# One scalar folded into the operations of a bias network, early loads moved, and the last sums cut in halves

## The chip, the cores and the metric

The kernel runs on one core of a Trainium2 chip. The metric is the device time of one execution in microseconds (us), as the median of several runs; less is better. The engines are TensorE (PE in the rows; its weight loads PEld), VectorE (DVE), ScalarE (ACT), GpSimd (POOL) and SyncE (SP), which issues nearly all transfers here.

## The reference

Attention with 4 batches, 8 heads, 576 positions and a head width of 64, in float32, with a learned bias on the scores; its output goes through two feed-forward layers. Cut to what matters here:

```python
scores = q @ k.T / sqrt(64)
x = log1p(abs(i - j)) / log1p(max(i, 1))           # per pair of positions
h = maximum(x[..., None] * w1 + b1, 0)             # 32 hidden units
scores += (h @ w2).transpose(2, 0, 1)              # one bias per head
attn = softmax(scores) @ v                         # then (2304, 512) tokens
x1 = hardswish(attn @ moe_w_in) @ moe_w_out        # 512 -> 2048 -> 512
out = sigmoid(x1 @ w_gate) * (x1 @ w_val) @ w_out  # 512 -> 1536 -> 512
```

## The kernel before

The bias stage comes first. The hidden layer is worked out on 128 partitions, 32 hidden units for each of four neighbouring rows i. `tbl` holds log1p of the distance; it is loaded in two pieces, the far one (columns `NEAR` on, 640 columns, needed first) and the near one (511 columns). `mlpc` holds w1, b1 and w2, `rows` the values of log1p(i) (`psi`) and 8 over it. L445 multiplies the two pieces of the table by w1 in place. L446 and L447 make `bpsi`, b1 times psi, with both signs. Dividing x by psi is put off: max(w1 * table + b1 * psi, 0) is the hidden value times psi. There are 36 groups `G` of 16 rows, each with four operations over 576 columns, one for each `ct`. In five of six groups the first of the four is done by ScalarE (L482, Relu with a bias per partition); the others are done by VectorE (L484, the maximum of the table and minus b1 * psi, with a correction `corr`, L459, added later). The results go round a ring of 12 buffers (`hids`), so that an operation of group G waits for the matmuls of group G - 3. TensorE multiplies by w2 (L489) into one of four PSUM tiles. `bias_out` then scales by 8 / psi and adds `corr` on ScalarE (L467) into one of three `p` buffers, and after every second group SP writes the pair to DRAM (`nbias`, L470). When all rows of a block of 128 are written, SP loads that block for the first pair of heads (`load_bias`, L219; the fifth, short block in two pieces, `bias_m`, L221 and L222). Three warm-up matmuls (L438) read a zeroed piece of the first ring buffer.

The attention has 16 units (pair of heads and batch), each with 9 steps; two steps make a slot (`slot_of_two`). A step forms scores on TensorE (L262), adds the bias on VectorE (L266), takes exp on ScalarE (L282, into the same three `p` buffers), and turns the result on TensorE (L320); later slots multiply by v (`av`, L352) and scale. The operands of the scores are split in a high and a low part by `prep`: for unit 0 it is ScalarE (casts, L230) and VectorE (L238), called within the bias stage behind groups 4 and 12; for the others ScalarE casts q (L230), and GpSimd rounds k (L234) and forms both low parts (L238). q and k of a unit are loaded by `load_qk` (L209 and, for the two halves of k, L211) into one buffer, so a load waits until `prep` has read the unit before. For unit 1 it is called behind the last group, after the last `nbias` write; for unit n + 1 later, a step after the second half of `prep` for unit n.

The feed-forward layers follow, with TensorE as the busy engine; the weights stream in behind it. At the very end three blocks of 128 rows are summed with the other half of the layer (L664, 512 columns) and written (L665), each as soon as its matmuls are through.

The planner of the framework chooses the order of the instructions of each engine within what they need of each other; `issue_after` is the one means by which the program fixes an order on a queue.

Of the kernel before, what the change touches and what calls it, by code (L numbers as in the profile page):

```python
# [13 lines left out]
AF = mybir.ActivationFunctionType  # L14
ALU = mybir.AluOpType
# [3 lines left out]
P = 128  # L19
# [7 lines left out]
TW = 384  # L27
# [6 lines left out]
ND, NPSI = 2 * S - 1, S // 4 + S // 16  # L34
NEAR = S - 65
# [60 lines left out]
def block_kernel(ctx: ExitStack, tc: tile.TileContext, q, k, v, mlp, w_in, w_out, w_gate, w_val, w_out2, dist_d,  # L96
                 rows_d, out):
    nc = tc.nc
# [9 lines left out]
    nbias = [dram.tile([min(P, S - P * c), H, S], F32, name=f"nbias{c}") for c in range(5)]  # L108
# [83 lines left out]
    q_in, k_in, bpsi, mlpc, rows = [early[:, i:j] for i, j in zip(cut, cut[1:])]  # L192
    k_in, bpsi = [a.rearrange("p (h s) -> p h s", h=2) for a in (k_in, bpsi)]
    bias_t = [apool.tile([P, 2, S], F32, name=f"bias{c}") for c in range(4)]
    bias_m = apool.tile([P, S], F32, name="bias_m")
# [8 lines left out]
    w1c, b1c, w2bd = mlpc[:, 0:1], mlpc[:, 1:3], mlpc[:, 3:35]  # L204
    corr = apool.tile([P, 2], F32, name="corr")

    def load_qk(n):
        qn[n], kn[n] = q_in[0:D], k_in
        nc.sync.dma_start(qn[n], q[n])  # L209
        for r in range(2):  # L210
            nc.sync.dma_start(kn[n][D * r : D * r + D], k[n])  # L211

    def load_v(n):
        vn[n] = a2.tile([P, 10, D], F32, name="vn")
        return nc.sync.dma_start(vn[n], v[n])

    def load_bias(p, c):
        if c < 4:
            nc.sync.dma_start(bias_t[c], nbias[c][:, 2 * p : 2 * p + 2, :])  # L219
        else:  # L220
            nc.sync.dma_start(bias_m[0:64], nbias[4][:, 2 * p, :])  # L221
            nc.sync.dma_start(bias_m[64:P], nbias[4][:, 2 * p + 1, :])  # L222

    def prep(n, h, on=PREP_ON):

        Q, K, qt, kt = Qs[n % 2][:, QH[h]], Ks[n % 2][:, :, h], qn[n][:, QH[h]], kn[n][:, h]

        def high(eng, out, x):
            if eng == "A":
                nc.scalar.copy(out, x)  # L230
            elif eng == "V":
                nc.vector.tensor_copy(out, x)
            else:
                nc.gpsimd.tensor_tensor(out=out, in0=x, in1=one[0 : x.shape[0]].to_broadcast(x.shape), op=ALU.mult)  # L234

        def low(eng, out, x, hi):
            eng = nc.vector if eng == "V" else nc.gpsimd
            eng.tensor_tensor(out=out, in0=x, in1=hi.bitcast(F32), op=ALU.subtract)  # L238

        high(on[0], Q[0:D], qt)  # L240
        high(on[1], K[:, 0], kt)
        low(on[2], Q[D:P], qt, Q[0:D])
        low(on[3], K[:, 1], kt, K[:, 0])
# [123 lines left out]
    for n in range(NU):  # L367
        i = (NSTEP * n + 5) // 2 + 2
        j = max(i + 2, (NSTEP * n + 8) // 2 + 2)
# [7 lines left out]
    def slot_of_two(i):  # L377

        for t in steps(i):
            scores(t)  # L380
            n, s = seq[t]
            p, b = divmod(n, B)
            if s == 0:
                last_v[0] = load_v(n)
            if b == B - 1 and p + 1 < NPAIR and (s % 2 == 1 or s == 8):
                load_bias(p + 1, s // 2)
        for n, a, g in AV.get(i, ()):
            av(n, a, g)
            if g == 4:
                av_out(n, a)  # L390
        for t in steps(i):
            expo(t)
        for t in steps(i - 1):
            n, s = seq[t]
            if s in (5, 8):
                invert(n, s // 6 * 3, s // 6 * 2 + 3)
        for t in steps(i - 2):
            n, s = seq[t]
            if s in (5, 8):
                turn_inv(n, s // 6 * 3, s // 6 * 2 + 3)  # L400
        for t in steps(i - 1):
            trans(t)
            n, s = seq[t]
            if s in REM:
                trans_rem(n, REM[s])
        for t in steps(i):
            if t in PREP:
                n, h = PREP[t]
                prep(n, h)
            for k, (n, h) in PREP.items():  # L410
                if h == 1 and n + 1 < NU and t == k + 3:
                    load_qk(n + 1)

    PREP = {}
    for n in range(1, NU):
# [3 lines left out]
    with ExitStack():  # L419

        tbl = x1[3][:, 0:ND]
        hids = [x1[i][:, S * j : S * j + S] for i in range(3) for j in range(4)]
        psi, rpsi8 = rows[:, 0 : S // 4], rows[:, S // 4 : NPSI]
        nc.sync.dma_start(mlpc, mlp)
        nc.sync.dma_start(rows, rows_d)
        nc.sync.dma_start(tbl[:, NEAR:ND], dist_d[:, NEAR:ND])
        nc.sync.dma_start(tbl[:, 0:NEAR], dist_d[:, 0:NEAR])

        warm = x1[0][:, 0:512]
# [11 lines left out]
        for i in range(2):  # L441
            nc.gpsimd.memset(Pm[i][:, 0:64], 0.0)

        for r in (slice(NEAR, ND), slice(0, NEAR)):
            nc.vector.tensor_scalar(out=tbl[:, r], in0=tbl[:, r], scalar1=w1c, scalar2=None, op0=ALU.mult)  # L445
        nc.vector.tensor_scalar(out=bpsi[:, 0], in0=psi, scalar1=b1c[:, 0:1], scalar2=None, op0=ALU.mult)  # L446
        nc.vector.tensor_scalar(out=bpsi[:, 1], in0=psi, scalar1=b1c[:, 0:1], scalar2=-1.0, op0=ALU.mult,  # L447
                                op1=ALU.mult)
# [7 lines left out]
        for ct in range(4):  # L456
            r = slice(32 * ct, 32 * ct + 32)
# [4 lines left out]
        def bias_out(G, ps):  # L462
            if G % 2 == 0:
                evs[0] = a2.tile([P, 2, S], F32, name="p", bufs=3)
            ev = evs[0]
            b = corr[:, 1:2] if G % ACT_SKIP == ACT_SKIP - 1 else corr[:, 0:1]
            nc.scalar.activation(halves(ev[:, G % 2]), ps[:, :, 0:HS], AF.Identity, bias=b, scale=rpsi8[:, G : G + 1])  # L467
            if G % 2 == 1:
                c, r = divmod(16 * (G - 1), P)
                last_b[0] = nc.sync.dma_start(nbias[c][r : r + 32].rearrange("(g i) h j -> (i h) g j", g=2), ev)  # L470
                if r == P - 32 or G == S // 16 - 1:
                    load_bias(0, c)
# [3 lines left out]
        for G in range(S // 16):  # L476
            hid = [hids[(4 * G + ct) % 12] for ct in range(4)]
            for ct in range(4):
                qd = 4 * G + ct
                src = tbl[:, S - 1 - 4 * qd : 2 * S - 1 - 4 * qd]  # L480
                if ct == 0 and G % ACT_SKIP != ACT_SKIP - 1:
                    nc.scalar.activation(hid[ct], src, AF.Relu, bias=bpsi[:, 0, qd : qd + 1], scale=1.0)  # L482
                else:
                    nc.vector.tensor_scalar(out=hid[ct], in0=src, scalar1=bpsi[:, 1, qd : qd + 1], scalar2=None,  # L484
                                            op0=ALU.max)
            ps = bp.tile([P, 2, 512], F32, name="s")
            for a in range(2):
                for ct in range(4):
                    nc.tensor.matmul(ps[32 * ct : 32 * ct + 32, a, 0:HS], w2bd, hid[ct][:, HS * a : HS * a + HS],  # L489
                                     start=True, stop=True)  # L490
            if pend is not None:
                bias_out(*pend)
            pend = (G, ps)
            if G in (4, 12):
                prep(0, G // 12, "AAVV")
        bias_out(*pend)
        with tc.issue_after(last_b[0].ins):
            load_qk(1)

        def split_x(x):  # L500
            for c in range(4):
# [133 lines left out]
        for j, (part2, t) in enumerate(todo):  # L635
            os = [mp.tile([P, 512], F32, name=f"o{c}") for c in range(NB)]
            prev = None
            for e in range(NH * part2, NH * part2 + NH):
                while load.done < 2 * NF + 3 * e + 3:
                    load.tick()  # L640
                s0 = 2 * NF + 3 * e
                pg = project(slots[s0 % NALL])
                pv = project(slots[(s0 + 1) % NALL])
                g = moe.tile([P, TW], F32, name="g", bufs=2)
                nc.scalar.activation(g, pg, AF.Sigmoid)  # L645
                nc.vector.tensor_tensor(out=g, in0=g, in1=pv, op=ALU.mult)  # L646
                gg = split_g(g)
                if prev is not None:
                    out2(e - 1, prev, os, e - 1 == NH * part2, False, False)
                prev = gg  # L650
                freed = 2 * NF + 3 * NH * part2
                if t == NTILE - 1:
                    freed += 3 * (e - NH * part2)
                if e % NH < NH - 2:
                    go_on(freed, 68)
            if j + 1 < len(todo):
                split_x([X2[:, c] for c in range(4)])
                if j + 2 < len(todo):
                    X2 = take(x2[todo[j + 2][1]])
            out2(NH * part2 + NH - 1, prev, os, False, True, j == len(todo) - 1)  # L660
            for i in range(NB):
                o = acc[NB * t + i]
                if part2:
                    nc.vector.tensor_tensor(out=o, in0=o, in1=os[i], op=ALU.add)  # L664
                    nc.sync.dma_start(out[TW * t + P * i : TW * t + P * i + P, :], o)  # L665
                else:
                    evac("AV"[i % 2], o, os[i])

# [26 lines left out]
```

## Time and profile before

| | |
|---|---|
| median of 3 runs | 1209.4 us (1208.53 to 1209.43) |
| profiled execution | 1207.13 us |
| its span | 1205.4 us |
| TensorE busy | 1187.5 us, 99% of the span |
| VectorE / ScalarE / GpSimd busy | 57% / 48% / 11% |
| granted TensorE clock | full in all 40 slices of the span |
| bias stage, first to last L484 | 5.59 to 59.43 us |
| last sum begins / span ends | 1201.65 / 1205.4 us |

Busy shares are averages over stages with different limits, and a busy TensorE is not one at its peak, since its matmuls overlap. So the stages are read one by one: in each, the engine whose rows follow each other with no idle time sets the length, and the others have room. A row of the timeline has start and duration, and several like instructions in a row are drawn together, with their count; the bracket behind it gives idle time of the engine before it and what ended it.

### The profile page before, as it was taken

What the parts mean: (1) busy time and instruction counts of PE and PEld (TensorE: products, weight loads), DVE (VectorE), ACT (ScalarE), POOL (GpSimd) and SP (SyncE); (2) the same over time, 40 slices, a digit from 0 to 9 for tenths busy, and PEclk for the clock granted to TensorE, in tenths of its full rate; (3) what the DMA queues carried; (4) which work ended last, traced back from release to release, by engine and by line L of the source; (5) the groups of instructions that cost most, each with busy time, mean ns of one, the idle gap of its engine ahead of it and who ended that gap; (6) DMA issues with size and microseconds to landing.
All of it is one profiled execution on the core that took longest, in us unless ns stands there. A gap on an engine that the chain in (4) does not pass through costs nothing.

```text
span 1205.4 us, 18764 instructions
## 1 busy us (share of the span) xinstructions
PE 1187.5 (99%) x7302; PEld 1057.4 (88%) x7302; DVE 682.1 (57%) x1464; ACT 574.2 (48%) x1224; POOL 133.2 (11%) x108
## 2 busy tenths in 40 slices
PE   8989999999999999999999999999999999999998
PEld 3467777777789999999999999999999999999998
DVE  8967887778876555645565545564431544222332
ACT  7978877877854444434344434333321332221221
POOL 0055545544200000000000000000000000000000
PEclk9999999999999999999999999999999999999999
DMA  6643635353211232212222223322210121101000
GB/s 210 244 141 105 186 100 178 110 164 108 76 53 67 92 105 80 79 62 80 74 69 82 92 88 114 122 80 79 64 58 1 62 79 53 53 1 53 27 27 27
DMA packets 36152, 106.76 MB, mean 89 GB/s; under 512 B 3936, under 2 KB 10336, under 8 KB 36064
## 3 DMA queue, kind: packets, MB, share of 16 engines
q1 hardware_dynamic: 36064, 105.57, 26.9%
q8 instruction: 57, 0.93, 0.3%
q14 instruction: 31, 0.25, 0.1%
HBM read 80.78 MB, written 24.77 MB: 88 GB/s over the span
## 4 chain that ended last, share of the span: by engine, by line
PE 87%; DVE 6%; ACT 3%; DMA 2%; issue 1%; POOL 0%; SPq 0%; DVEq 0%; ACTq 0%
PE o L574 16%; PE h L512 13%; PE h L510 13%; PE h L511 13%; PE o L631 12%; PE s L262 6%; PE av L352 5%; PE tr L320 4%; PE s L489 1%; PE av L355 1%; DVE u L266 1%; DVE x L484 1%; DVE z L143 1%; ACT p L282 1%; PE tr L299 1%
## 5 line engine op out<-in xcount | busy, mean ns | idle before, releaser
L510 PE MATMUL h<-early,slot 128*128 128x384 f32 x952 | 318.9, 335 | 0.0
L512 PE MATMUL h<-early,slot 128*128 128x384 f32 x952 | 318.8, 335 | 0.0
L511 PE MATMUL h<-early,slot 128*128 128x384 f32 x952 | 318.5, 335 | 0.0
L510 PEld LDWEIGHTS h<-early,slot 128*128 128x128 f32 x952 | 178.8, 188 | 2.6
L511 PEld LDWEIGHTS h<-early,slot 128*128 128x128 f32 x952 | 178.7, 188 | 2.5
L512 PEld LDWEIGHTS h<-early,slot 128*128 128x128 f32 x952 | 178.7, 188 | 0.1
L551 ACT CAST gh<-g 128x384 fp32r<-128x384 f32 x166 | 85.0, 512 | 162.4 <-DVE g L646 119.8
L574 PE MATMUL o<-gh,slot 128*128 128x384 f32 x768 | 156.9, 336 | 3.0 <-ACT raw L310 1.8
L646 DVE TENSOR_TENSOR g<-g,h 128x384 f32<-128x384 f32 x72 | 39.8, 553 | 183.1 <-PE h L512 183.1
L574 PEld LDWEIGHTS o<-gh,slot 128*128 128x128 f32 x768 | 134.2, 188 | 6.9 <-ACT raw L310 4.4
L552 DVE TENSOR_TENSOR gl<-g,gh 128x384 fp32r<-128x384 f32 x166 | 92.2, 558 | 79.1 <-ACT gh L551 77.0
L516 ACT ACTIVATE g<-h,half 128x384 f32<-128x384 f32 x94 | 54.5, 580 | 131.1 <-PE h L512 127.5
L262 PE MATMUL s<-k,q 128*128 128x288 f32 x640 | 112.2, 310 | 2.5 <-POOL k L234 1.2
L645 ACT ACTIVATE g<-h 128x384 f32<-128x384 f32 x72 | 35.4, 492 | 165.0 <-PE h L512 165.0
L282 ACT ACTIVATE p<-u,stat 128x576 f32<-128x576 f32 x128 | 98.7, 773 | 28.9 <-DVE stat L266 28.5
L631 PE MATMUL o<-slot,gh 128*128 128x512 f32 x432 | 111.9, 393 | 0.0
L266 DVE CUSTOM_DVE_ANT_0 u<-s,bias 128x576 f32<-128x576 f32 x128 | 93.5, 753 | 24.9 <-PE s L262 24.3
L517 DVE SCALAR_TENSOR_TENSOR g<-g,h 128x384 f32<-128x384 f32 x94 | 51.8, 552 | 95.2 <-ACT g L516 95.1
L262 PEld LDWEIGHTS s<-k,q 128*128 128x128 f32 x640 | 89.0, 189 | 5.9 <-POOL k L234 1.7
L631 PEld LDWEIGHTS o<-slot,gh 128*128 128x128 f32 x432 | 80.1, 188 | 13.6 <-issue 0.2
L574 PE MATMUL o<-gl,slot 128*128 128x384 f32 x384 | 88.5, 334 | 0.0
L352 PE MATMUL av<-ptm,vn 128*64 128x288 f32 x512 | 78.9, 419 | 1.2 <-DVE x L359 0.7
(99 smaller groups left out, 1494.0 us busy)
## 6 DMA issues: line engine op xcount, KB each, us to landing
raw<-in_part_dram SPq DMA_DIRECT2D x68, 512.0 KB, 3.5
nbias<-p SPq DMA_DIRECT2D x18, 576.0 KB, 3.2
early<-in_part_dram SPq DMA_DIRECT2D x32, 288.0 KB, 4.3
bias<-nbias SPq DMA_DIRECT2D x16, 576.0 KB, 6.0
take<-x SPq DMA_DIRECT2D x12, 768.0 KB, 4.1
vn<-in_part_dram SPq DMA_DIRECT2D x16, 320.0 KB, 3.1
early<-in_part_dram SPq DMA_DIRECT2D x16, 304.0 KB, 3.8
part<-raw SPq DMA_DIRECT2D x12, 384.0 KB, 2.6
```

What stands on the lines that cost most here:

```text
L262: nc.tensor.matmul(ps[:, a, 0:HS], Q[:, q0 : q0 + P], K[:, r, h, HS * a : HS * a + HS], start=(i == 0), stop=(i == len(mm) - 1))
L266: last_u[0] = nc.vector.tensor_tensor_reduce(out=halves(u), in0=ps[:, :, 0:HS], in1=halves(bt), op0=ALU.add, op1=ALU.min, scale=-0.125, sc ...
L282: nc.scalar.activation(probs(t), us.pop(t), AF.Exp, bias=low[n % 2][:, s : s + 1], scale=-1.0, accum_out=sums[n % 3][:, s : s + 1])
L352: nc.tensor.matmul(ps[64 * h : 64 * h + 64, 0:HS], vt[:, 4 * h + g], ptm[:, h, g, cols], start=(g == 0), stop=False)
L510: nc.tensor.matmul(ps[:, 0:TW], wh, XH[:, c], start=(c == 0), stop=False)
L511: nc.tensor.matmul(ps[:, 0:TW], wl, XH[:, c], start=False, stop=False)
L512: nc.tensor.matmul(ps[:, 0:TW], wh, XL[:, c], start=False, stop=(c == 3))
L516: nc.scalar.activation(g, ph, AF.Relu, bias=half, scale=1.0 / 6.0)
L551: nc.scalar.copy(gh, g)
L552: last_g[0] = nc.vector.tensor_tensor(out=gl, in0=g, in1=gh.bitcast(F32), op=ALU.subtract)
L574: nc.tensor.matmul(os[c][:, 0:TW], sl[:, r, P * c : P * c + P], x, start=(first and r == 0 and x is gh), stop=(last and x is gl))
L631: nc.tensor.matmul(os[i], x[:, P * i : P * i + P], sl[:, r], start=(first and x is gh and r == 0), stop=(end and x is gl))
```

## The change

The two multiplications L445 are taken out. w1 becomes the scale of ScalarE's Relu (L482) and the first of two operations in VectorE's L484: multiply by w1, then take the maximum; both read w1 as a scalar per partition, beside the one that they read already. `mlpc` and `rows` are loaded from ScalarE's queue, and the far piece of the table is the first load on SP. q and k of unit 1 are loaded at group 31, behind the latest `nbias` write issued by then (that of groups 28 and 29). The later calls of `load_qk` are held behind the second half of the latest load of `bias_m`. In the last tile each sum and its write are made in two halves of 256 columns.

```diff
+    last_m = [None]
     def load_bias(p, c):
...
-            nc.sync.dma_start(bias_m[64:P], nbias[4][:, 2 * p + 1, :])
+            last_m[0] = nc.sync.dma_start(bias_m[64:P], nbias[4][:, 2 * p + 1, :])
...
                 if h == 1 and n + 1 < NU and t == k + 3:
-                    load_qk(n + 1)
+                    with tc.issue_after(last_m[0].ins):
+                        load_qk(n + 1)
...
-        nc.sync.dma_start(mlpc, mlp)
-        nc.sync.dma_start(rows, rows_d)
         nc.sync.dma_start(tbl[:, NEAR:ND], dist_d[:, NEAR:ND])
+        nc.scalar.dma_start(mlpc, mlp)
+        nc.scalar.dma_start(rows, rows_d)
         nc.sync.dma_start(tbl[:, 0:NEAR], dist_d[:, 0:NEAR])
...
-        for r in (slice(NEAR, ND), slice(0, NEAR)):
-            nc.vector.tensor_scalar(out=tbl[:, r], in0=tbl[:, r], scalar1=w1c, scalar2=None, op0=ALU.mult)
...
-                    nc.scalar.activation(hid[ct], src, AF.Relu, bias=bpsi[:, 0, qd : qd + 1], scale=1.0)
+                    nc.scalar.activation(hid[ct], src, AF.Relu, bias=bpsi[:, 0, qd : qd + 1], scale=w1c)
                 else:
-                    nc.vector.tensor_scalar(out=hid[ct], in0=src, scalar1=bpsi[:, 1, qd : qd + 1], scalar2=None,
-                                            op0=ALU.max)
+                    nc.vector.tensor_scalar(out=hid[ct], in0=src, scalar1=w1c, scalar2=bpsi[:, 1, qd : qd + 1],
+                                            op0=ALU.mult, op1=ALU.max)
...
+            if G == 31:
+                with tc.issue_after(last_b[0].ins):
+                    load_qk(1)
         bias_out(*pend)
-        with tc.issue_after(last_b[0].ins):
-            load_qk(1)
...
                 if part2:
-                    nc.vector.tensor_tensor(out=o, in0=o, in1=os[i], op=ALU.add)
-                    nc.sync.dma_start(out[TW * t + P * i : TW * t + P * i + P, :], o)
+                    for c in (slice(0, 256), slice(256, 512)) if j == len(todo) - 1 else (slice(0, 512),):
+                        nc.vector.tensor_tensor(out=o[:, c], in0=o[:, c], in1=os[i][:, c], op=ALU.add)
+                        nc.sync.dma_start(out[TW * t + P * i : TW * t + P * i + P, c], o[:, c])
```

## Rows read from the trace of the kernel before

**Rows 1.** The page, busy time of TensorE (us, share of the span, instructions).

```profile
PE 1187.5 (99%) x7302; PEld 1057.4 (88%) x7302; DVE 682.1 (57%) x1464; ACT 574.2 (48%) x1224; POOL 133.2 (11%) x108
```

**Rows 2.** Stretches: length, busy (instructions) per engine, clock, DMA share, GB/s.

```profile
70.90:84.00 13.10, 10.83 (x64) 6.63 (x64) 5.34 (x15) 7.91 (x21) 9.27 (x8) 1.00 0.45 113
110.60:118.40 7.80, 7.80 (x63) 5.69 (x64) 6.07 (x16) 6.11 (x17) 7.15 (x6) 1.00 0.08 12
```

**Rows 3.** Timeline of VectorE, 2 to 60 us: start, duration, engine, line, operation, count.

```profile
5.00 0.55 DVE L445 TENSOR_SCALAR x<-x,early 128x640 f32<-128x640 f32 x1 [1.08 <-DMA x<-in_part_dram]
...
6.03 0.49 DVE L445 TENSOR_SCALAR x<-x,early 128x511 f32<-128x511 f32 x1
...
7.21 0.66 DVE L459 TENSOR_SCALAR corr<-s 32x1 f32<-32x1 f32 x4 [0.26 <-PE s L454]
7.90 5.68 DVE L484 TENSOR_SCALAR x<-x,early 128x576 f32<-128x576 f32 x13
...
27.96 31.47 DVE L484 TENSOR_SCALAR x<-x,early 128x576 f32<-128x576 f32 x73
```

**Rows 4.** Timeline of VectorE, from 352 us: two operations with immediates alone.

```profile
352.34 0.75 DVE L141 TENSOR_SCALAR z<-z 128x512 int32<-128x512 int32 x2
353.01 1.29 DVE L143 SCALAR_TENSOR_TENSOR z<-raw,z 128x512 int32<-128x512 int32 x2
```

**Rows 5.** Timeline of ScalarE, 14 to 20 and 68 to 70 us.

```profile
15.56 1.43 ACT L482 ACTIVATE x<-x,early 128x576 f32<-128x576 f32 x2
...
18.93 1.54 ACT L467 ACTIVATE p<-s,corr,early 128x576 f32<-128x576 f32 x2
...
68.42 0.58 ACT L310 COPY ptm<-tr 128x512 f32<-128x512 f32 x1
68.90 0.26 ACT L310 COPY ptr<-tr 128x128 f32<-128x128 f32 x1
69.05 0.67 ACT L230 CAST q<-early 64x576 fp32r<-64x576 f32 x1
69.63 0.78 ACT L282 ACTIVATE p<-u,stat 128x576 f32<-128x576 f32 x1
```

**Rows 6.** Groups by line and form: busy us, mean ns, idle before.

```profile
L664 DVE TENSOR_TENSOR x<-x,o 128x512 f32<-128x512 f32 x16 | 10.1, 683 | 9.3 <-PE o L631 9.3
```

**Rows 7.** Timeline of SP, 0 to 110 us: issues of transfers.

```profile
0.74 0.38 SPq L424 DMA_DIRECT2D early<-in_part_dram  x1
...
1.64 0.42 SPq L426 DMA_DIRECT2D x<-in_part_dram  x1
...
51.79 7.64 SPq L470 DMA_DIRECT2D nbias<-p  x4
...
67.16 0.46 SPq L221 DMA_DIRECT2D bias_m<-nbias  x1
...
68.30 1.24 SPq L211 DMA_DIRECT2D early<-in_part_dram  x2
```

**Rows 8.** Timeline of GpSimd, 60 to 90 us.

```profile
73.35 2.25 POOL L234 TENSOR_TENSOR k<-early,one 128x576 fp32r<-128x576 f32 x2 [1.76 <-DVE stat L288]
75.56 2.77 POOL L238 TENSOR_TENSOR k<-early,k 128x576 fp32r<-128x576 f32 x2
```

**Rows 9.** Timeline of TensorE, 68 to 120 us: matmuls with v.

```profile
70.89 0.70 PE L352 MATMUL av<-ptm,vn 128*64 128x288 f32 x2 [0.53 <-DVE ptm L312]
...
84.04 1.68 PE L352 MATMUL av<-ptm,vn 128*64 128x288 f32 x12
...
110.55 1.68 PE L352 MATMUL av<-ptm,vn 128*64 128x288 f32 x12
...
118.32 1.68 PE L352 MATMUL av<-ptm,vn 128*64 128x288 f32 x12
```

**Rows 10.** One line of the kernel, L288: duration in ns, least, median and most.

```profile
L288 DVE TENSOR_SCALAR stat<-stat x32: 160/172/1380, 68.9 to 337.1; 128x6 f32<-128x6 f32 x16, 128x3 f32<-128x3 f32 x16
```

**Rows 11.** Issues of transfers by line: count, KB each, median us to landing.

```profile
early<-in_part_dram SPq DMA_DIRECT2D x32, 288.0 KB, 4.3
```

## The prediction

> **What bounds the kernel now.** Read the busy line of the page first [rows 1]: TensorE works 99% of the span, so outside of a few stretches nothing but its own work counts, and an edit pays only where TensorE waits. Next take the stretches by engine [rows 2]. From 70.9 to 84.0 us TensorE has 64 matmuls in 13.1 us; from 110.6 to 118.4 it has 63 in 7.8 us. The first stretch is the entry of the second unit. Third, the timeline of VectorE for the first 60 us [rows 3]: from 7.90 on, the operations of L484 run with no row's idle time named between them until 59.43 (27.96 + 31.47), 112 of the 114, with four subtractions of `prep` in the gaps. VectorE sets the length of the bias stage; TensorE and ScalarE wait on it there. So two stretches are open, the bias stage (VectorE) and the entry of unit 1 (its operands), and the last microseconds after the last matmul.
>
> **The sum's base.** The profiled execution took 1207.13 us, of which the span is 1205.4; the median shown is 1209.4, 2.3 above it. I work out differences on the span and put them on the median. A measurement of this kernel can tell about 0.2%, 2.4 us, from no change.
>
> **w1 inside the operations.** (a) The two multiplications of L445 go. Before them VectorE waits 1.08 for the far half of the table, until 5.00 [rows 3]; the table is sent third on SP, at 1.64, and is there 3.36 us later. Sent first it leaves 0.9 earlier (1.64 - 0.74 [rows 7]) and is there near 4.1. The small tables come on ScalarE's queue at about the old times, and the `bpsi` operations end near 3.9 as now (5.00 - 1.08), so L484 starts at 4.1. L459 still waits for the warm-up matmuls and begins at 7.2 [rows 3]. (b) Each L484 gets a second per-partition scalar read from SBUF. No row of this kernel shows VectorE with two. The bounds: the nearest row without any, L141 with two immediates, starts one per 0.335 us at 512 columns (two from 352.34 to 353.01) [rows 4]; by the slope between L445's 640 and 511 columns (0.55 and 0.49, about half a nanosecond a column) [rows 3] 576 columns would take some 0.033 more, 0.368. L484 with one scalar starts one per 0.430 us (31.47 less one duration of 0.52, over 72) [rows 3]. One scalar costs 62 ns. The second costs 0 if it is read beside the first, 62 if behind it. ScalarE shows which is nearer: a copy of 576 columns from SBUF gives way to its successor after 0.58 (69.05 to 69.63) and L482 with one scalar after 0.67 (1.43 - 0.76), so one costs 0.09; a copy of 512 columns out of PSUM gives way after 0.48 (68.42 to 68.90), which is at most 0.54 for 576, and L467 with two, out of PSUM, after 0.71 (1.54 - 0.83), so two cost at least 0.17 [rows 5]. There they add up. I take the additive 62 ns, because ScalarE's rows are the nearest that show two, and keep 0 and 31 for the rivals. A gain is excluded: the operation streams the same 576 columns and reads one operand more.
>
> So on VectorE before: 7.90 + 112 x 0.430 + 3.37 = 59.43. After: between 4.1 and 7.2 six operations fit at 0.492, L459 ends at about 7.87, then 108 x 0.492 + 3.37 bring 64.4. That is **+4.9 us**; if L459 is placed ahead of more of them and VectorE waits for the warm-up, up to +6.0 (two L484 fewer before it). The order within an engine is chosen by the planner, so this is open.
>
> (c) ScalarE: L482 gets its second scalar too, 30 x 0.09 = 2.8 us. In six groups ScalarE then has 5 x 0.76 + 6 x 0.72 = 8.1 us and VectorE 19 x 0.492 = 9.3. It hides under VectorE: **0**. If the second scalar is free on VectorE (19 x 0.43 = 8.2), this cover is gone, the two are level, and about 1 us of the gain is lost.
>
> **Two queues.** Costed in (a). ScalarE issues two DMAs of some 0.4 us before its first work, while nothing else waits for it until 4.1: 0.
>
> **q and k of unit 1 behind group 31.** Now q goes out after the last group; the two halves of k go at 68.30, behind the two loads of `bias_m`, which hold the queue until 67.16 because the last `nbias` write must land first [rows 7]. A load of a half of k lands in 4.3 us (median) [rows 11]; GpSimd starts on k at 73.35, when the scores of unit 1 are next on TensorE [rows 8]. The cost: from the first `av` matmul of unit 0's first half to the first of its second half, 70.89 to 84.04, 13.15 us; the same two slots of unit 2, 110.55 to 118.32, take 7.77 [rows 9]. **-5.4 us** if q and k are ready. What is late next: GpSimd needs 2.25 + 2.77 for k and about as much again for q's two low parts as for k's, 8 us [rows 8]. Sent behind the write of groups 28 and 29 (the second of the four that begin at 51.79, near 54 [rows 7]), q and both halves of k leave within about 2 us and land near 60, and GpSimd ends near 68, before 74.5, so it hides. Should ScalarE keep its casts of q where they are (the second at 69.05 [rows 5]), q's low part comes 1 us late: -4.4. In the other direction GpSimd no longer holds VectorE at 68.9, where an L288 took 1.38 instead of its median 0.17 [rows 10], and ScalarE may do its casts in the idle time before the scores: up to -1.2 more. Range -4 to -6.6. Queued on SP behind the moved loads are the `nbias` writes of groups 31, 33 and 35; the first of them goes out near 56.6, about when the moved issues end, so none is held up at the issue; the three loads ahead of them (288 KB for each half of k [rows 11], about as much for q) can delay a landing by some 2 us, which costs up to 1 us at the first `exp`, whose output buffer the write of groups 30 and 31 still reads. The guard on later units, behind `bias_m`'s second half, costs nothing: from unit 2 on these loads wait for GpSimd.
>
> **Last sums in halves.** A 512-column sum takes 0.683 [rows 6]; a half takes between 0.34 (all of it data) and 0.45 (some 0.1 of start added to each). The last pair ends 0 to 0.2 later than the whole did; the last transfer is half as large, but SP issues six instead of three, at about 0.4 each. Between -0.2 and +0.4: **+0.1**.
>
> **Sum, the forecast.** 4.9 - 5.4 + 0.1 = -0.4: **1209.0**, with its own range -3 to +2.5, 1206.4 to 1211.9. The gain at the second unit is paid away in the bias stage.
>
> **Rivals.** (1) The second scalar is free. VectorE ends at 7.87 + 107 x 0.43 + 3.37 = 57.3, -2.2, of which ScalarE takes back up to 1: -1.2 to -2.2, with the rest -6.5 to -7.5, about **1202.4**. For it: an instruction could fetch both scalars at once; against it: ScalarE's rows. Beside it stands the Trainium skill, VectorE: DVE Perf Modes, section on the TRN2 errata, whose table gives a VectorE operation 58 cycles plus the columns over the mode's factor and no term for scalars; by that L484 would take 360 ns per start before and after. The trace disagrees for L484 (430 ns) and agrees for the operation with immediates (327 against 335), so that rule has no price for a scalar, and this rival's chance rests on ScalarE's rows alone. (2) Half price, 31 ns: VectorE ends near 60.9, +1.5, sum -3.8: **1205.6**. (3) The other side: GpSimd's preparation meets the tail of the L484s. A VectorE operation of the kind of L484 that meets a GpSimd operation waits for its end, as L288 does, 1.38 instead of 0.17 [rows 10]. If k lands 1 us or more before the last L484, GpSimd's four k operations (2.25 + 2.77) alternate with two to four L484, each of which waits some 1.2: +2.4 to +4.8, with the rest about **1212.6**. It decides from there because k lands 6 us after its turn, and VectorE has 5.5 us (6.3 at 0.492) left: by my numbers they just miss. The Trainium skill, SBUF — State Buffer, speaks of the same thing in its part on the shared port pair, an exclusive lock that the second of the two waits out in full; the trace agrees at L288. (4) The loads are not early after all, or another operand is late at 70 to 80 (`bias_m`, the casts), and the entry of unit 1 stays slow: +4.9 + 0.1, **1214.4**.
>
> **Chances.** Forecast 0.45, (1) 0.30, (2) 0.09, (3) 0.12, (4) 0.04. Faster by over 2.4 us: all of (1), most of (2), 0.02 of the forecast: 0.40. Slower: (4), most of (3), 0.04 of the forecast: 0.17. Within: 0.43. The range takes in most of (1) and half of (3), 1201.5 to 1212.5.
>
> **What would show it.** In the changed kernel's VectorE timeline: the distance of two L484 (0.430, 0.461 or 0.492), the start of the first (4.1), the end of the last (64.4 in the forecast, 57.3 in (1)); single L484 of over 1 us beside GpSimd would be (3). On TensorE: the distance between the two `av` starts of unit 0 (7.8 instead of 13.15). On SP: k before the write of group 31. After the last matmul: the last landing within 0.4 of now. The prediction is wrong if L484 keeps 0.43, or if the two `av` starts stay over 10 us apart.

## The result, and the profile after

The changed kernel takes 1224.14 us (1220.09 to 1226.15), beside 1208.99 for the kernel before on the same chip: the ratio is 1.013, with an interval of 1.0113 to 1.0147. It is slower by some 15 us, and the time lies outside the predicted range. Its profiled execution, the slowest of its four, took 1226.15, with a span of 1224.4, so 19.0 more than that of before. (One of the nine executions of the kernel without the guard, further below, took 3976.38 us at a granted clock of 0.291 and stands outside the range given there.) The page's busy line of after answers to [rows 1]:

```profile
PE 1197.5 (98%) x7302; PEld 1060.7 (87%) x7302; DVE 681.6 (56%) x1465; ACT 576.7 (47%) x1224; POOL 133.5 (11%) x108
```

TensorE has 10 us more of busy time for the same 7302 matmuls, at a mean granted clock of 0.993 instead of 1.000, and stood idle for 9 more. Both kernels have the same matmuls, in the same order but for some 70 places, so the k-th matmul of one trace can be set against the k-th of the other. This table gives by how much each kernel's matmul starts later than that of before (us), at the times of before in the first column. The columns besides "after" are kernels of the next section; the guard is the part of the change that holds the later calls of `load_qk` behind the second half of `bias_m`.

```
at      after  no guard  guard alone  early q,k  fold alone  fold+early
 50      4.35      4.29       -0.06      -0.72        3.65        3.99
 70      6.35      6.29       -0.07      -0.10        5.36        5.99
 95      1.63      2.02        0.40      -4.39        3.57        1.71
149      2.19      2.03        0.33      -3.15        4.21        1.74
165      7.67      2.02        5.68      -3.16        4.21        1.74
204      9.18      1.99        5.80      -3.18        4.21        1.74
240     12.41      2.19       11.04      -3.21        4.20        2.04
290     14.99      2.19       12.43      -3.22        4.21        2.07
314     19.25      2.19       17.19      -3.20        4.20        2.10
1195    18.50      2.13       18.68      -3.56        4.99        3.02
```

Read down the column "after". The bias stage loses 6.35, the entry of unit 1 gives 4.7 back, as was forecast in kind. Then, from 149 to 314 us, where the prediction has nothing, 17 us go, in steps: 13 of them near 152, 224 and 296 us of the first column, the other 4 near 206 and 275. The feed-forward layers give 0.75 back and the last sums cost 0.5: 19.0 in all.

**The bias stage.** Timeline of VectorE in after (start, duration, engine, line, count, idle time before); it answers to [rows 3], with the lines one or two numbers higher (L485 is the former L484, L460 the former L459):

```profile
5.11 0.30 DVE L447 TENSOR_SCALAR early<-early 128x144 f32<-128x144 f32 x1 [3.69 <-DMA early<-in_part_dram]
5.32 0.29 DVE L448 TENSOR_SCALAR early<-early 128x144 f32<-128x144 f32 x1
5.65 2.54 DVE L485 TENSOR_SCALAR x<-x,early 128x576 f32<-128x576 f32 x5
8.11 0.65 DVE L460 TENSOR_SCALAR corr<-s 32x1 f32<-32x1 f32 x4
...
29.68 35.91 DVE L485 TENSOR_SCALAR x<-x,early 128x576 f32<-128x576 f32 x73
```

Two L485 stand (35.91 - 0.58) / 72 = 0.491 us apart (0.58 is the duration of one; 0.492 was forecast), and the last ends at 65.59 (forecast 64.4). The first starts at 5.65 and not at 4.1: VectorE waits 3.69 for the small tables.

**The entry of unit 1.** Timeline of TensorE in after; it answers to [rows 9]. From the first `av` to the one of the second half there are 8.52 us, before 13.15:

```profile
77.17 0.70 PE L354 MATMUL av<-ptm,vn 128*64 128x288 f32 x2
...
85.69 1.68 PE L354 MATMUL av<-ptm,vn 128*64 128x288 f32 x12
```

TensorE is busy for all of this stretch of after (columns as in [rows 2]):

```profile
77.17:85.69 8.52, 8.52 (x61) 5.81 (x60) 5.38 (x14) 6.61 (x18) 2.72 (x3) 1.00 0.38 87
```

**The new loss.** First SP's issues around a change of head pair, in the kernel before, where the loads are those of unit 5 (the same comes back for units 9 and 13); there q goes out at 116.44 and k at 117.94 and 119.35, ahead of most of the bias loads (L219):

```profile
116.44 0.48 SPq L209 DMA_DIRECT2D early<-in_part_dram  x1
117.94 0.47 SPq L211 DMA_DIRECT2D early<-in_part_dram  x1
118.91 0.33 SPq L219 DMA_DIRECT2D bias<-nbias  x1
119.35 1.25 SPq L211 DMA_DIRECT2D early<-in_part_dram  x1
...
127.75 0.59 SPq L222 DMA_DIRECT2D bias_m<-nbias  x1
131.21 1.11 SPq L211 DMA_DIRECT2D early<-in_part_dram  x2
...
142.54 0.33 SPq L215 DMA_DIRECT2D vn<-in_part_dram  x1
142.93 0.42 SPq L127 DMA_DIRECT2D raw<-in_part_dram  x1
```

The same in after. The guard puts q and k (L209, L211) behind `bias_m` (L223, L224), so they leave at 130.37 and 131.01:

```profile
129.69 0.59 SPq L224 DMA_DIRECT2D bias_m<-nbias  x1
130.37 0.55 SPq L209 DMA_DIRECT2D early<-in_part_dram  x1
131.01 1.19 SPq L211 DMA_DIRECT2D early<-in_part_dram  x2
141.66 0.47 SPq L209 DMA_DIRECT2D early<-in_part_dram  x1
146.76 1.11 SPq L211 DMA_DIRECT2D early<-in_part_dram  x2
147.96 0.54 SPq L215 DMA_DIRECT2D vn<-in_part_dram  x1
148.54 0.42 SPq L127 DMA_DIRECT2D raw<-in_part_dram  x1
```

In the kernel before these loads do wait for GpSimd, which still reads the unit before out of the same buffer, but only until 117.91:

```profile
116.49 1.42 POOL L238 TENSOR_TENSOR k<-early,k 128x576 fp32r<-128x576 f32 x1
```

Then they leave at once, some ten microseconds ahead of `bias_m` (second half at 127.75). The guard makes them wait for `bias_m`'s turn as well. The rest follows on the queue. GpSimd prepares unit 5 that much later and is through with k at 146.7 in after:

```profile
143.93 2.81 POOL L240 TENSOR_TENSOR k<-early,k 128x576 fp32r<-128x576 f32 x2
```

Only then may the next k (146.76, before 131.21) overwrite it; and behind this waiting load stand v and the next raw feed-forward weights (`raw`, L127), which leave at 148.54 instead of 142.93. They land at 155.9, and ScalarE has stood there since 150.92:

```profile
155.93 0.67 ACT L133 ACTIVATE z<-raw 128x512 f32<-128x512 f32 x1 [5.01 <-DMA raw<-in_part_dram]
```

The late issue is only a part of this: the load also takes longer to land, 7.4 us in after (issues of 146 to 152 us) against 3.9 in before (issues of 142 to 148 us; KB each, us to landing):

```profile
raw<-in_part_dram SPq DMA_DIRECT2D x1, 512.0 KB, 7.4
```

```profile
raw<-in_part_dram SPq DMA_DIRECT2D x1, 512.0 KB, 3.9
```

Both halves of k, v, raw and the next q leave within four us there, and the DMA engines are busy for 0.93 of 150 to 155 us. At the two later places it is 6.0 and 7.1 us against 4.2 and 3.8. Waits of after from 145 to 172 us (who, for whom, us in total, times, longest):

```profile
ACT z L133 <- DMA raw<-in_part_dram: 5.0, 1, 5.0
...
PE tr L322 <- DVE ptm L314: 4.4, 1, 4.4
DVE z L134 <- ACT z L133: 4.4, 1, 4.4
```

ScalarE stands 5.0 us at the conversion of weights that the feed-forward layers read some 200 us later, with the exp of the running unit behind it; VectorE stands at the next step of the same conversion, with the copy `ptm` behind it; and TensorE waits for that copy. Nothing on this path is urgent but its place in three queues. The stretches of after (length, busy time and instructions by engine, clock, DMA share, GB/s) show what it does to TensorE and its clock:

```profile
150.00:155.00 5.00, 3.89 (x31) 2.60 (x29) 1.98 (x5) 0.92 (x4) 3.30 (x4) 1.00 0.93 248
155.00:160.00 5.00, 1.68 (x8) 1.68 (x9) 3.27 (x7) 2.81 (x8) 2.29 (x2) 0.58 0.32 82
160.00:165.00 5.00, 5.00 (x30) 3.32 (x30) 2.95 (x9) 2.46 (x7) 0.00 (x0) 0.74 0.21 48
```

### The profile page after: what moved, and what is told of

The parts are those of the page before. It is cut to its first block, busy times and chain, and to the rows that moved or that the text cites. A ratio compares the mean times of both kernels' runs of the same rounds, so it can differ in the third digit from the quotient of the medians.

```text
span 1224.4 us, 18770 instructions
## 1 busy us (share of the span) xinstructions
PE 1197.5 (98%) x7302; PEld 1060.7 (87%) x7302; DVE 681.6 (56%) x1465; ACT 576.7 (47%) x1224; POOL 133.5 (11%) x108
## 4 chain that ended last, share of the span: by engine, by line
PE 86%; DMA 5%; DVE 3%; ACT 2%; POOL 2%; issue 1%; SPq 0%; DVEq 0%; ACTq 0%; POOLq 0%
PE o L576 16%; PE h L514 13%; PE h L512 13%; PE h L513 13%; PE o L633 12%; PE s L264 5%; PE av L354 5%; PE tr L322 3%; DMA raw<-in_part_dram 3%; PE s L490 2%; PE av L357 1%; DVE x L485 1%; DMA nbias<-p 1%; DMA x<-raw 1%; PE tr L301 1%
## 5 line engine op out<-in xcount | busy, mean ns | idle before, releaser
L322 PE MATMUL tr<-ident,p 128*128 128x128 f32 x512 | 73.2, 277 | 11.1 <-DVE ptm L314 11.1
```

The source lines that it names most:

```text
L322: nc.tensor.transpose(ps[:, kc], pts[n, c][:, h, 64 * h + P * kc : 64 * h + P * kc + P], ident)
```

## The experiments

Theory 1 says that the guard makes the new loss, by the way just read; theory 2 that the loss comes from the other parts of the change and the guard is as harmless as the prediction had it.

**The guard taken out of the changed kernel.**

```diff
-                    with tc.issue_after(last_m[0].ins):
-                        load_qk(n + 1)
+                    load_qk(n + 1)
```

> The changed kernel without the guard: the loads of q and k of a unit are no longer held behind the second half of the load of bias_m; all other edits stay. Theory 1 (the guard): in the changed kernel TensorE falls back by 4 to 7 us three times, near 152, 224 to 233 and 285 to 311 us, each time behind a late load on SP, and until then it is only 2.2 us behind. Without the guard the three losses go and the kernel ends some 1 to 3 us over the kernel before: 1209 to 1212. Theory 2 (the bias stage and the earlier k shift the later work against each other): the three losses stay, 1220 to 1226.

Measured: 1212.96 (1209.81 to 1214.15), ratio 1.0038, 1.0027 to 1.0048. The steps are gone (table, "no guard"): the kernel is 2.0 behind at 95 us and 2.1 at the end.

**The guard alone**, in the kernel before.

> The kernel before with the guard alone. Theory 1: the three losses come back without any of the other edits, 5 to 7 us each, so 1222 to 1228. Theory 2: nothing happens, 1209, as the guard only names an order that the queue keeps anyway.

Measured: 1224.57, ratio 1.0137, 1.0117 to 1.0157. The steps come back at the same places, to 17.2 at 314 us. Theory 2 falls: the guard costs 16.2 us by itself.

**The early loads alone**: `load_qk(1)` at group 31, nothing else.

> The kernel before with q and k of unit 1 loaded at group 31 and nothing else. My account of the entry of unit 1: the distance between the two av starts of unit 0 falls from 13.15 to 8 or 8.5 us, and the kernel gains 4 to 5 us: 1204 to 1205. Rival: GpSimd's preparation meets the tail of the bias stage and takes the gain back: 1207 to 1211, with single operations of L484 of over 1 us.

Measured: 1203.28 (1202.9 to 1203.91), ratio 0.9963, 0.9948 to 0.9977. The two starts of `av` are 70.71 and 79.66, 8.95 apart, so 4.2 less than before. What is late next is seen on VectorE in this run: `bias_m` itself, which SP could only load at 68.22, and an L288 that meets GpSimd:

```profile
71.85 0.76 DVE L266 CUSTOM_DVE_ANT_0 u<-s,bias_m 128x576 f32<-128x576 f32 x1 [2.07 <-DMA bias_m<-nbias]
...
74.72 1.40 DVE L288 TENSOR_SCALAR stat<-stat 128x3 f32<-128x3 f32 x1
```

**The fold alone**: w1 inside L482 and L484, the multiplications L445 out, the loads as before.

> The kernel before with w1 folded into the operations of the bias stage and nothing else. Two L484 start 0.492 us apart instead of 0.430; 114 times 0.062 is 7.1 us, of which the two multiplications taken out and the earlier start give back 1 to 2: the scores begin 5 to 6 us later and the kernel takes 1213.5 to 1215.5, as nothing behind the stage makes up for it. If the later stall at unit 1 swallows a part of it, 1211 to 1213.

Measured: 1213.76, ratio 1.0053, 1.0037 to 1.007. VectorE in this run; the table, not the small tables, ends the wait for the first L482, at 4.79:

```profile
3.61 0.30 DVE L444 TENSOR_SCALAR early<-early 128x144 f32<-128x144 f32 x1 [2.18 <-DMA early<-in_part_dram]
...
4.79 2.05 DVE L482 TENSOR_SCALAR x<-x,early 128x576 f32<-128x576 f32 x4 [0.69 <-DMA x<-in_part_dram]
...
28.98 35.92 DVE L482 TENSOR_SCALAR x<-x,early 128x576 f32<-128x576 f32 x73
```

**What the 61 ns (0.491 - 0.430) are for**: two operations, but one scalar.

```diff
-    nc.vector.tensor_scalar(out=hid[ct], in0=src, scalar1=bpsi[:, 1, qd : qd + 1], scalar2=None, op0=ALU.max)
+    nc.vector.tensor_scalar(out=hid[ct], in0=src, scalar1=1.0, scalar2=bpsi[:, 1, qd : qd + 1],
+                            op0=ALU.mult, op1=ALU.max)
```

> The kernel before, with L484 as two operations and one scalar: multiply by the immediate 1.0, then maximum with the one per-partition scalar. The values are the same. The changed kernel's L485 has two operations and two scalars and started one per 0.492 us instead of 0.430. Theory A, the price is the second scalar read from SBUF: the pitch stays 0.430, the last L484 ends near 59.4, the time is 1208.4 within 1. Theory B, the price is the second arithmetic step: the pitch is 0.492, 62 ns on 114 operations, of which the L484 after the start at 5.6 all count, so that the last ends near 66 and the time is about 1214.5.

Measured: 1208.31, ratio 1.0006, 0.9994 to 1.0017. The row is that of before, to a hundredth:

```profile
28.00 31.47 DVE L484 TENSOR_SCALAR x<-x,early 128x576 f32<-128x576 f32 x73
```

So the second arithmetic step is free and the second scalar read from SBUF costs the 61 ns (theory A).

**The queues alone.**

```diff
-        nc.sync.dma_start(mlpc, mlp)
-        nc.sync.dma_start(rows, rows_d)
         nc.sync.dma_start(tbl[:, NEAR:ND], dist_d[:, NEAR:ND])
+        nc.scalar.dma_start(mlpc, mlp)
+        nc.scalar.dma_start(rows, rows_d)
```

> The kernel before, with the far half of the table first on SP and the small tables on ScalarE's queue; the multiplications of L445 stay. Theory A, the second queue makes the small tables later: in the changed kernel they were there at 5.1 (the first bpsi operation). L445 then starts at 5.1, the first L484 about 1.0 later than that and two short bpsi operations more, near 6.7 instead of 5.59, and with VectorE as the bound of the bias stage the time is 1.0 to 1.5 above the kernel before, 1209.6. Theory B, the table was the late one, as the prediction said: L445 starts near 4.1, and the time is 0.9 lower, 1207.5. If neither shows more than 0.5, the queues are out as a part of the difference between the run without the guard (1212.96) and the sum of the fold and the early loads (about 1208.6).

Measured: 1208.22, ratio 1.0008, 0.9999 to 1.0017: neither theory's size. VectorE shows why; both of them hold in part:

```profile
4.12 0.55 DVE L445 TENSOR_SCALAR x<-x,early 128x640 f32<-128x640 f32 x1 [2.70 <-DMA early<-in_part_dram]
4.98 0.30 DVE L446 TENSOR_SCALAR early<-early 128x144 f32<-128x144 f32 x1 [0.30 <-DMA early<-in_part_dram]
```

The table is there at 4.1, as forecast, but the larger of the small tables, needed by the next operation, is there at 4.98, where the fold alone had it at 3.61. On ScalarE's queue the two small loads took 3.2 and 3.8 us from issue to landing in after, on SP's queue 1.7 and 2.1 before. What one load wins the other loses.

**The halves alone.**

> The kernel before with only the last pair of sums in halves. The prediction gave it -0.2 to +0.4. Nothing above 0.6 either way is expected of it by any theory: what is left of the difference between the run without the guard and the sum of its parts lies elsewhere if this holds. If it costs 1 to 4 us, the halves are where that difference comes from: 1210 to 1212.

Measured: 1208.57, ratio 1.0009, 1.0 to 1.0018. In the trace the last matmul begins at 1201.87 and the span ends at 1206.5, 4.6 later; before, 1201.22 and 1205.4, 4.2: +0.4 to +0.5. SP now has four issues for the last two blocks in place of two:

```profile
1202.28 1.87 SPq L666 DMA_DIRECT2D out_dram<-acc  x4
```

**The guard, with the raw weights on ScalarE's queue.** The next runs ask how the guard costs. In this one the raw weights no longer stand behind k on SP.

```diff
-                nc.sync.dma_start(raw, self.todo[i].bitcast(I32))
+                (nc.scalar if i < NPRE else nc.sync).dma_start(raw, self.todo[i].bitcast(I32))
...
-                with tc.issue_after(last_v[0].ins):
+                with tc.issue_after(last_v[0].ins), tc.issue_after(exps[-4].ins):
```

> The kernel before with the guard, as in the run of the guard alone (1224.57), but the raw weights that are loaded beside the attention go out on ScalarE's queue, behind an exp two slots back, and so no longer stand behind the held k load on SP; v still does. Theory A, the time is lost because the raw weights stand behind the k load that waits for GpSimd, and ScalarE, VectorE and then TensorE wait for them: the steps of +4 to +5 us at 150, 225 and 306 us shrink to under 1.5 each, and the time is 1208 to 1213. Theory B, the late k itself (or v) holds TensorE: the steps stay, 1222 to 1226. In between, the steps halve: both count. ScalarE issues each of these loads itself, some 0.4 us each, 7 of them.

Measured: 1227.31, ratio 1.0162, 1.0148 to 1.0176. The time is that of theory B, but not the steps. At the places of the guard's three steps the lag now stands still (5.3 at 146 and at 158 us of the table's first column, 13.3 and 13.0 at 218 and 230, 19.3 at 290 and 302), and others have come: from 1.6 to 5.3 between 128 and 140, from 8.0 to 13.3 between 200 and 212, from 15.7 to 19.2 between 266 and 284. The rows of ScalarE show that the experiment moved the wait and did not take it away:

```profile
128.85 0.36 ACTq L127 DMA_DIRECT2D raw<-in_part_dram  x1
...
137.16 0.67 ACT L133 ACTIVATE z<-raw 128x512 f32<-128x512 f32 x1 [3.56 <-DMA raw<-in_part_dram]
138.46 0.72 ACT L232 CAST q<-early 64x640 fp32r<-64x640 f32 x1 [0.64 <-DMA early<-in_part_dram]
```

The raw weights now leave at 128.85, in the midst of `bias_m`, q and k, and all of them land late: the issues of 128 to 140 us have 8.3 us to landing for raw, 8.4 for q and 8.5 for k, where the median of the early loads was 4.3 [rows 11]. ScalarE waits for raw 11.4 us between 110 and 320 us, and 8.2 for q. The Trainium skill, DMA: Bandwidth & Descriptors, in the section Issuing engines are not separate DMA queues, says that transfers from any engine end on the same 16 DMA engines and interleave; these landings agree.

**The guard, with three raw loads out of its way.** The three loads of raw weights that stood right behind the held k loads go out at the end of the attention instead; and the same without the guard as its measure.

```diff
-            if i % EVERY == 0 and i > 10 and load.n < NPRE:
+            if (i % EVERY == 0 and i > 10 and i not in (24, 42, 60) or i in (68, 69, 70)) and load.n < NPRE:
```

> The kernel before with the guard, and the three loads of raw weights that stand right behind the held k loads (146.7, 221.5 and 298.1 us in the run of the guard alone) are taken from there and go out at the end of the attention, where no load is held. To be read against the next run, which has the same three loads late and no guard. Theory A, the guard costs its 16 us because these three loads land late and ScalarE stands at them: the guard costs under 5 here, so under 5 above the next run. Theory B, the late q and k hold ScalarE, GpSimd or TensorE by themselves, as the waits for q (9.3 us in all) in the run with the raw weights on ScalarE's queue hint: the guard still costs 10 or more.

> The kernel before without the guard, with the same three loads of raw weights moved to the end of the attention. The measure for the run above. At the end of the attention three loads and their three conversions come on top: by the rows of before at that place between 0 and +6 us.

Measured: with the guard 1209.16 (ratio 1.0013, 1.0002 to 1.0024), without it 1205.6 (0.9979, 0.997 to 0.9988). The guard costs 3.6 us here, and 16.2 with these loads in their place. Waits of ScalarE for raw, 110 to 320 us, first in the run of the guard alone, then with the loads moved:

```profile
ACT z L133 <- DMA raw<-in_part_dram: 17.2, 6, 5.0
```

```profile
ACT z L133 <- DMA raw<-in_part_dram: 4.0, 3, 1.8
```

Without the guard no such wait is listed. So some 12.6 of the 16.2 us go by the raw weights behind the held k, as theory A has it.

**The guard on q alone.**

> The kernel before with the guard on the loads of q only; the loads of k go out in their old order, from unit 2 on. If the whole cost comes by k (GpSimd prepares k first, the next unit's k waits for that, and v and the raw weights stand behind it), this one costs under 4: 1208 to 1212. If q's delay alone is enough, since ScalarE casts q and GpSimd takes its low part, 1216 or more. About half would say that both count.

Measured: 1213.36 (ratio 1.0039, 1.0023 to 1.0055), +5.3: between the two, nearer to the first. ScalarE waits 5.6 us for raw in it, for the loads that leave ahead of `bias_m` (issued at 124.23, 196.42 and 266.81) and not for those behind the held ones. A late q costs 5.3 us, a late q and k 16.2.

**The guard on unit 2 alone, with the early loads.**

> The early q and k loads alone gave 1203.28. There unit 2's q (63.1 us) stood ahead of bias_m (68.2) on SP. This kernel is the kernel before with the early loads and with the guard on unit 2's loads only, the one place where a load of q stands right ahead of bias_m; units 5, 9 and 13 keep their early places. If bias_m's place is worth anything at the entry of unit 1, the two starts of av come closer than the 8.95 us of the early loads alone, towards 8.0, and the time is 1202.5; if not, 1203.3, the same. If the guard costs at unit 2 what it costs at units 5, 9 and 13, some 5 us each, the time is 1208.

Measured: 1203.63 (ratio 0.9968, 0.9955 to 0.998), the same as the early loads without it, so at unit 2 the guard costs nothing. It moves little there: k goes out at 69.87 instead of 69.41, the raw weights behind the next k at 86.73 instead of 85.72, and ScalarE, which comes to them at 95.47, waits for none. In the trace the two starts of `av` are 8.52 apart, VectorE waits 1.41 us for `bias_m` instead of 2.07, and the L288 that took 1.40 takes 0.16; the times do not show this gain.

**The changed kernel, with the three raw loads moved.**

> The changed kernel, guard included, with the three loads of raw weights that stood right behind the held k loads moved to the end of the attention. If what the guard costs there is what it cost beside the kernel before (16.2 with these loads in their place, 3.6 with them moved), this gives the run without the guard, less 2.5 for the move, plus 3.6: 1212.96 - 2.5 + 3.6 = about 1214, from 1224. If the changed kernel has another cause, the time stays above 1220.

Measured: 1207.48, ratio 0.9997, 0.9987 to 1.0008: 16.7 us less than the changed kernel, by moving three loads. It is lower than the 1214 that the medians add up to, by 6.5. On the traces the lags at 314 us do add: 2.19 without the guard, -2.74 for the moved loads, +1.37 for the guard beside them make 0.82, and 1.05 is seen. At the end they do not: 2.13, -1.45 and +2.33 make 3.0, and -0.39 is seen, so some 3.4 of the miss arise after 314 us. The median of the run without the guard stands 3.2 above its own profiled execution, which is about the rest. Why is open for both. Stretches of this run, where after had clocks of 0.93 and 0.78:

```profile
230.00:235.00 5.00, 5.00 (x43) 4.74 (x43) 4.12 (x10) 4.22 (x12) 2.60 (x3) 1.00 0.59 190
306.00:312.00 6.00, 6.00 (x47) 4.77 (x45) 3.46 (x11) 5.49 (x17) 3.80 (x3) 1.00 0.01 3
```

**Fold and early loads together.**

> The kernel before with w1 inside the operations and the early q and k loads, without the guard, the two queues and the halves. Alone the two gave +5.4 and -5.1, so if they add 1208.6. If the longer bias stage takes part of the early loads' gain away, as the run without the guard suggests (1212.96, of which the queues and the halves alone gave 0.4 and 0.8), 1211 to 1212.

Measured: 1210.94, ratio 1.002, 1.0011 to 1.003, +2.8 where the two alone make +0.3. The table shows a part of it: with the fold alone the lag falls from 5.36 at 70 us to 3.57 at 95 by itself, as if the slow entry of unit 1 hid 1.8 of it. With the early loads that cover is gone: together the lag falls by 4.28 between 70 and 95 us, just what the early loads give alone (4.29), and the 1.8 is not had a second time. But of the 2.5 us by which the lags miss adding at 95 us only 0.7 is left at 149, and 1.6 at the end, so this is argued and not shown. Queues and halves, +0.4 (within its interval nothing) and +0.8 alone, then lead to within 0.8 of the 1212.96 without the guard.

**The version that is left**: the kernel before, with the early loads and the three raw loads moved.

> The kernel before with the early q and k loads (1203.3 alone) and the three loads of raw weights moved to the end of the attention (-2.5 alone). The two act in different stages, 75 to 85 us and from 150 us on, so they should add: 1200.8. If the move only removed small waits that the early loads remove as well: 1203.

Measured: 1200.87 (1199.82 to 1201.89), ratio 0.9935, 0.9918 to 0.9953. The two gains add, and it beats both kernels.

## Why the prediction was wrong

**The failed step** is the sentence "The guard on later units, behind `bias_m`'s second half, costs nothing: from unit 2 on these loads wait for GpSimd." No group of rows stands behind it. The second half of it was true and did not carry the first: GpSimd is through at 117.9, and `bias_m` goes out at 127.3, so at units 5, 9 and 13 the guard is the later of the two. The term that was put at nothing is 16.2 us (guard alone). Of what stands behind these loads on SP the prediction named nothing: next come the next unit's q and k, v and raw weights, and with three of the raw loads moved the price is 3.6. How the other 3.6 divide between late q, late k and the waits for raw that are left (4.0 us on ScalarE) was not settled. Neither of the signs that the prediction had named as its refutation occurred (L484 at 0.43, `av` starts over 10 us apart): none of them looked at the later units.

**The front of the bias stage** was a smaller miss. "The small tables come on ScalarE's queue at about the old times" failed: the first `bpsi` operation began at 5.11 instead of 3.42 and the second ended at 5.61 instead of 3.9, so L484 began at 5.65 and not 4.1, and the last ended 1.2 later than forecast. The far table at 4.1 was right.

**Right.** The second scalar at an additive 62 ns: 61 were measured, 0.491 apart, and with two operations and one scalar 0.430. Rivals 1 and 2 fall with it. The table in the section on the TRN2 errata of the Trainium skill's page VectorE: DVE Perf Modes, with no term for scalars, does not fit what was measured (0.430 and 0.491). The entry of unit 1: 13.15 to 8.52, -4.6, within -4 to -6.6 and short of the -5.4 taken by 0.75. In after this rest is no wait: TensorE is busy for all 8.52 us, with as many matmuls (60 begin in either) as in the 7.77 of unit 2, but it takes the first twelve `av` in two pieces, 2 at 77.17 and 10 at 78.27, which [rows 9] show as one piece of 12. That the prediction counted the whole difference to unit 2 as waiting was its error here. `bias_m`, which rival 4 named, is late where unit 2's loads are not held (2.07 us in the early loads alone, with 8.95 between the two `av`), and it decides less than that rival held. Rival 3 did not occur: GpSimd begins at 65.05, at the end of the L485s, and no L485 took over 1 us. Halves: forecast -0.2 to +0.4, in the traces +0.4 to +0.5, in the median +0.8. Two slips of the working move nothing: 30 x 0.09 is 2.7 and not 2.8, in a term that counts 0, and rival 2 ends at 61.0 and not 60.9.

**The sum.** Without the guard the changed kernel's matmuls are 2.0 behind at 95 us, where 4.9 - 5.4 = -0.5 was forecast: the bias stage cost 6.3 and not 4.9, and the entry of unit 1 gave 4.3 back and not 5.4. The halves add 0.5. By the medians the forecast was 4.0 low on this part (1212.96 against 1209.0), which is just outside its range too, and 15 low with the guard.

## What to carry to other kernels

Before a load is tied behind another, look at when it leaves now, unit by unit, not at one unit that stands for all; and list what stands behind it on its queue. Here a load that waited (k, 146.76 instead of 131.21) held the later ones of its queue (raw, 148.54 instead of 142.93), and a conversion that nobody needed for some 200 us stopped three engines for 5.0, 4.4 and 4.4 us, because it was next in their order. Of the 16.2 us, 12.6 were mended at the far end, by moving the unhurried loads out of the hurried stretch of the queue; moving them to another queue, where the transfers fell together with others, did not help (1227.31).

Folding a per-partition scalar into an operation that already reads one was not free: the second arithmetic step cost nothing, but the second scalar 61 ns on each of 114 operations.

## What the runs showed of the hardware

- VectorE with 576 columns of float32: 0.430 us apart with one scalar per partition, with one operation or two; 0.491 with two scalars. The difference is the read of the second scalar.
- Two small loads (17.5 and 90 KB) on a second queue, beside a 320 KB load on the first, took 3.2 and 3.8 us to land (after); ahead of it on one queue 1.7 and 2.1 (before).
- After TensorE had stood for 4.4 us, until 158.32, its granted clock in after was 0.58 over 155 to 160 us and 0.74 over 160 to 165. In the run of the guard alone, where it had stood for 4.0 us until 156.06, it was 0.50, which is the lower of its two levels (1.2 of 2.4 GHz), for a whole stretch of 5 us, though TensorE was busy for 3.94 of them (columns as above):

```profile
150.00:155.00 5.00, 2.03 (x18) 1.34 (x16) 1.31 (x3) 1.61 (x4) 4.95 (x4) 0.91 0.50 163
155.00:160.00 5.00, 3.94 (x17) 2.94 (x19) 4.30 (x11) 2.44 (x8) 0.02 (x1) 0.50 0.50 123
```
